# PSUM banks of the last two steps of the first stage, order of two copies, and due times of the output weights in an attention and spectral filter kernel

## The chip, the cores and the metric

The kernel runs on one core of one Trainium2 chip. The metric is the device time of one execution in microseconds (us). The engines are named as in the profile: PE multiplies matrices, PEld is its weight load, DVE is the vector engine, ACT the activation engine, POOL and SP issue most of the transfers (DMA); POOL computes a little too.

## The reference

Two independent halves, joined along the last axis. S = 2048, D = 448, 16 heads of 28, with one key and one value head for all:

```python
q = (x @ wq).reshape(B, S, H, Dh).transpose(0, 2, 1, 3)
k, v = x @ wk, x @ wv                       # one head of 28
p = softmax(einsum("bhqd,bkd->bhqk", q, k) * Dh ** -0.5)
a = einsum("bhqk,bkd->bhqd", p, v).transpose(0, 2, 1, 3).reshape(B, S, H * Dh) @ wo
X = rfft2(B_x, axes=(-2, -1)) * (w_r + 1j * w_i)
b = irfft2(X, s=(S, D), axes=(-2, -1))
out = concatenate([a, b], axis=-1)
```

## The kernel before

**First stage (0 to about 60 us).** The projections of queries, keys and values, and the first part of the spectral transform. Its tasks are declared with `add(engine, duration, function, *dependencies)`, and a small planner puts them in an order by these hand-written durations. [...] `spin(...)` hands out banks 0 to 5 in turn; banks 6 and 7 hold the two halves of the first transform (`fft1_mm`), which `fft1_evict` (L201) copies out, partly on ACT. The last two PE tasks of this stage are `turn_values_all` (16 transposes of the values, L616, into one bank) and `last_features` (L639; `features`, L184: the matmuls of the last features of the spectral block L = 3, two times 226 columns). PE then passes a branch on a register (L650), whose rare path widens the range of the numbers and is not taken here. Behind the branch DVE copies the turned values to `vs` (L722), makes the low half of the second half of the keys (`keys_low(1)`, L507; queue SP then copies them into place, L511), and copies the features to `late["a", 3]` (L726, a tile that the trace names `spoh`).

**Main loop.** 16 groups, one for each of 4 column chunks by 4 groups of heads, each of 16 steps over the keys: 256 steps. A step has two score units (`scores(i)`, L1326: 8 matmuls into two banks), two exponentials on ACT (L1329, 128 x 1024 each) and one value unit (`values(st)`, L1345: 8 matmuls that add into one bank). Score unit i uses the bank pair

```python
b = 2 * (2 * i % 3)          # L1321: banks 0/1, 4/5, 2/3, 0/1, ...
```

and the value unit of group n uses bank 7 − n % 2. The other of banks 6 and 7 is free for fillers. A filler is a piece of the spectral half or of the output product, put between units of attention when the kernel's own clocks allow: `late_features` (L1058), `late_points` (L1091), `late_top` (L1012), then `z_unit` (L1162), `y_unit` (L1188) and the output product (L1264). DVE copies each filler's bank out (L1067 and L1068, L1100 or L1102, L1017), and that sets when the bank is free for the next.

**Order of the side work.** `after(when, duration, function)` puts an event in a queue sorted by time on the kernel's own clock for DVE; `vector(until)` takes events out when they are due and emits their instructions. That clock is counted from the start of the main loop in assumed durations. Each engine and each DMA queue then runs its instructions strictly in the emitted order. The events that the change touches:

- `wo_load(g)` (L770): one part of the output weights by POOL's queue into one of two buffers; `wo_split(g)` (L773, and L775 for g < 4): its high and low half on DVE. Seven parts.
- `spread(i)` (L807): four transfers of the first spectral points into tile X, by POOL's queue; `first_points`: two reductions over X (L898, `peaks<-X`) and first butterflies (L822), some us later on DVE.

Beside them on POOL's queue: `weight_top` (L903, the spectral weights, whose largest value L898 takes), and for every finished group L1224 (sums to memory, after L1219 on DVE has taken them out of PSUM), L1225 (back in another layout, after the first has landed), L1230 and L1232 (their reciprocals, L1229, spread out).

Of the kernel before, what the change touches and what calls it, by code (L numbers as in the profile page):

```python
# [26 lines left out]
NG = 4  # L27
# [17 lines left out]
class Plan:  # L45
# [4 lines left out]
    def add(self, eng, dur, f, *deps, kb=0, due=None):  # L50
        t = {"eng": eng, "dur": dur, "f": f, "deps": [d for d in deps if d], "kb": kb, "due": due, "n": len(self.tasks)}
        self.tasks.append(t)
        return t
# [48 lines left out]
def kernel(ctx: ExitStack, tc: tile.TileContext, t: dict):  # L102
    nc = tc.nc
# [20 lines left out]
    bank = [banks[:, i] for i in range(8)]  # L124
    turn = count()

    def view(b, *dims):
        n = int(np.prod(dims))
        names = "abc"[:len(dims)]
        return b[:, :n].rearrange(f"p ({' '.join(names)}) -> p {' '.join(names)}", **dict(zip(names, dims)))  # L130

    def spin(*dims):
        return view(bank[next(turn) % 6], *dims)

    L = 3
    SEQ = 5, 6, 4, 7
    late, cs1 = {}, spare[1][1][:, :452].rearrange("p (j n) -> p j n", j=4)
# [40 lines left out]
    def features(pa, f, p, es=(0, 1)):  # L178
        for e in es:
            for k in range(2):  # L180
                for h in range(2):
                    for r in range(2):
                        r0 = 64 * h + 32 * r
                        mm(pa[r0:r0 + 32, e, 113 * k:113 * k + 113], f[:113, 2 * r + k, 2 * p + e, h], cs1[:113, 2 * r + k],  # L184
                           start=True, stop=True)
# [58 lines left out]
    with tc.tile_pool(name="f1", bufs=2) as f1[0], tc.tile_pool(name="w1", bufs=1) as w1, ExitStack() as ctx1:  # L244
# [10 lines left out]
        PE, DVE, ACT, SP, POOL = "PE", "DVE", "ACT", "SP", "POOL"  # L255
        add = plan.add

        kfz = add(POOL, 1.8, lambda: nc.gpsimd.memset(kf, 0.0))
        users = []
# [151 lines left out]
        fold, fa, ev_a, fm, outs, stores, xbl = {}, {}, {}, {}, {}, {}, {}  # L411
# [23 lines left out]
        pas = {}  # L435
# [18 lines left out]
        pbs, bst, store_tasks = {}, {}, {}  # L454
# [46 lines left out]
        def keys_cast(h, eng):  # L501
            hs = slice(h * 1024, h * 1024 + 1024)
            cast(eng, lambda: ka[:32, hs], lambda: kf[:32, hs])

        def keys_low(h):
            hs = slice(h * 1024, h * 1024 + 1024)
            nc.vector.tensor_tensor(ka[64:96, hs], kf[:32, hs], ka[:32, hs], op=ALU.subtract)  # L507

        def keys_twice(h, p):
            hs = slice(h * 1024, h * 1024 + 1024)  # L510
            nc.sync.dma_start(ka[64 * p + 32:64 * p + 64, hs], ka[64 * p:64 * p + 32, hs])  # L511
# [100 lines left out]
        turned = []  # L612

        def turn_values(bs):
            for b in bs:
                nc.tensor.transpose(turned[0][:, b], kf[32:64, b * 128:(b + 1) * 128], cons["ident"][32:64, 32:64])  # L616

        def turn_values_all():
            turned.append(next(turn) % 6)
            turned.insert(0, view(bank[turned[0]], 16, 32))  # L620
            turn_values(range(16))
            small["rv"] = nc.values_load(bits.bitcast(I32)[0:1, 0:1])
# [7 lines left out]
        def tops():  # L630
# [3 lines left out]
                         cm, ident_)  # L634
        fm_task(2)
        add(PE, 1.2, turn_values_all, users[-6], ident_, *krow_, *fetched["v"], bt_)
        users.append(None)

        def last_features():  # L639
            pas[L, 1] = spin(2, 226)  # L640
            features(pas[L, 1], ff[L], 1)
        add(ACT, 1.0, lambda: keys_cast(1, ACT), krow_[0], *fetched["k1"], bt_)
        add(PE, 0.8, last_features, users[-6], *store_tasks[L - 1])
        plan.run({PE: 4.4, DVE: 1.0, ACT: 2.0, SP: 0.6, POOL: 0.6})
        mask, ident = cons["mask"], cons["ident"]
        ctx1.close()
# [73 lines left out]


        nc.vector.tensor_copy(vs, turned[0])  # L722
        keys_low(1)
        for p in range(2):
            keys_twice(1, p)
        nc.vector.tensor_copy(late["a", L][:, 1], pas[L, 1])  # L726

    pp = ctx.enter_context(tc.tile_pool(name="pp", bufs=PAIRS))
    ap = ctx.enter_context(tc.tile_pool(name="ap", bufs=2))
# [10 lines left out]
    def after(when, dur, f, *a):  # L740
        heapq.heappush(events, (when, next(serial), dur, f, a))
# [609 lines left out]
            after(clk["pe"] + 0.4, 0.72, group_out, c, g)  # L1351

    for g in range(7):
        at = 24.0 + 6 * g if g < NG else 60.0 + 6 * g
        after(at, 0.0, wo_load, g)
        after(at + 6.0, 1.1, wo_split, g)

    last = acc(15)
    parts, tail = deque((k, g) for k in range(4) for g in range(NG - 1)), {}
# [10 lines left out]

    after(1.0, 0.0, largest)
    for i in range(4):
        after(30.0 + i, 0.0, spread, i)
    after(34.0, 0.0, first_points)
    after(20.0, 0.0, weight_top, 0)
    work["l"].extend([late_points(L, 0), late_points(L, 1)])
    late_load(0, "C")
# [49 lines left out]
    c, g = NC - 1, NG - 1  # L1427
# [150 lines left out]
```

## Time and profile before

| | |
|---|---|
| median of 3 runs | 580.16 us (580.13 to 581.7) |
| the profiled execution | 579.96 us |
| its span, first to last instruction | 578.2 us |
| mean granted clock of PE | 0.997 |
| main loop, first score matmul | 60.61 us |
| last value unit of the attention ends, by the chain of waits | 565.3 us |

The profile has one execution. Times in it are counted from the span's start. "Busy" leaves out waiting. In a group's line the number behind the second bar is the idle time of the engine ahead of these instructions, with what ended most of it. In a row of the timeline, the bracket is the idle time just ahead of it and its releaser. PEld runs beside PE, so its idle time is seldom a loss.

### The profile page before, as it was taken

The page shows a single profiled execution, that of the slowest core. Times are in us where ns is not written, and L with a number is a line of the kernel's source. Part 1 is how long each engine was busy: PE and PEld are TensorE (multiplying, and loading weights), DVE is VectorE, ACT ScalarE, POOL GpSimd, SP SyncE. Part 2 cuts the span into 40 slices and gives each one's busy share as a digit, 9 for nine tenths or more (in the row PEclk, how much of TensorE's full clock was granted, in tenths as well). Part 3 has the DMA queues.
Part 4 walks back from the last instruction along what each step waited for, and adds up shares of the span by engine and source line. Part 5 has one row for each costly group of instructions (what it writes and reads, how often), then busy time and mean ns, then how long its engine had stood idle before and what let it go on. Part 6 is the DMA issues. An engine that isn't in the chain of part 4 may idle for free.

```text
span 578.2 us, 21096 instructions
## 1 busy us (share of the span) xinstructions
PE 568.2 (98%) x9165; PEld 297.0 (51%) x9165; DVE 412.0 (71%) x779; ACT 510.1 (88%) x575; POOL 108.9 (19%) x199
## 2 busy tenths in 40 slices
PE   9999899899999999999999999999999999999997
PEld 7877344445554444444444444444555555554554
DVE  5994779799631899999899797873356743365566
ACT  4645799799999999999999999999999978899982
POOL 1024111122213012122111121032313212020200
PEclk9999899999999999999999999999999999999999
DMA  8843864424535302143411021267333323221112
GB/s 299 302 143 89 258 174 166 117 62 124 163 89 178 132 19 66 44 122 98 123 33 58 19 82 28 74 247 219 110 113 105 118 93 101 73 74 58 46 50 101
DMA packets 38359, 66.01 MB, mean 114 GB/s; under 512 B 6996, under 2 KB 28508, under 8 KB 38256
## 3 DMA queue, kind: packets, MB, share of 16 engines
q1 hardware_dynamic: 29432, 38.66, 20.7%
q0 software_dynamic: 8688, 25.76, 14.8%
q8 instruction: 72, 1.18, 0.8%
q14 instruction: 23, 0.19, 0.1%
q10 hardware_dynamic: 144, 0.23, 0.1%
HBM read 43.92 MB, written 19.97 MB: 111 GB/s over the span
## 4 chain that ended last, share of the span: by engine, by line
PE 83%; DVE 3%; DMA 1%; ACT 1%; issue 1%; POOL 0%; ACTq 0%; DVEq 0%; POOLq 0%
PE banks L1326 37%; PE banks L1345 36%; PE banks L1264 6%; PE banks L1162 2%; PE banks L1188 2%; PE banks L1091 1%; PE banks L1058 1%; DMA sd<-qraw 1%; DVE peaks L898 1%; ACT p L1329 1%; DMA wo<-wo 0%; DVE mt L1008 0%; ACT yb L1276 0%; DVE ka L507 0%; DVE spoh L1042 0%
## 5 line engine op out<-in xcount | busy, mean ns | idle before, releaser
L1329 ACT ACTIVATE p<-banks 128x1024 f32<-128x1024 f32 x512 | 476.5, 1085 | 27.7 <-PE banks L1326 26.4
L1326 PE MATMUL banks<-qa,ka 128*32 128x512 f16 x4096 | 275.0, 380 | 2.2 <-DVE spoh L726 2.2
L1345 PE MATMUL banks<-p,vs 128*32 128x512 f32 x2048 | 267.4, 592 | 0.3 <-DVE spol L1068 0.3
L1326 PEld LDWEIGHTS <-ka 128*32 128x32 f16 x4096 | 126.5, 97 | 168.6 <-issue 119.9
L1345 PEld LDWEIGHTS banks<-p,vs 128*32 128x32 f32 x2048 | 68.0, 110 | 44.4 <-issue 1.2
L1264 PE MATMUL banks<-woh,o 128*32 128x448 f16 x464 | 39.8, 352 | 0.0
L1232 POOL DMA_DIRECT2D R<-rd x60 | 30.3, 513 | 32.8 <-DMA rd<-rs 32.6
L1264 PEld LDWEIGHTS <-o 128*32 128x32 f16 x720 | 22.2, 97 | 27.1 <-issue 19.3
L864 DVE SCALAR_TENSOR_TENSOR X<-w,X 128x226 f32<-128x226 f32 (+2 forms) x72 | 34.0, 473 | 2.4
L1224 POOL DMA_DIRECT2D sd<-qraw x15 | 9.0, 598 | 126.9 <-DVE qraw L1219 126.9
L1269 DVE TENSOR_SCALAR ya<-banks,scales 128x448 f32<-128x448 f32 x12 | 8.2, 684 | 30.0 <-PE banks L1264 30.0
L1219 DVE TENSOR_SCALAR qraw<-banks,scales 128x512 f32<-128x512 f32 x15 | 11.2, 749 | 22.1 <-PE banks L1345 22.1
L1195 DVE TENSOR_SCALAR w<-banks,scales 128x256 f32<-128x256 f32 x16 | 7.7, 484 | 26.3 <-PE banks L1188 26.3
L1264 PE MATMUL banks<-wol,o 128*32 128x448 f16 x256 | 24.2, 352 | 0.0
L352 PE MATMUL banks<-xh,wqh 128*128 128x512 f32 x64 | 24.1, 408 | 0.0
L356 ACT ACTIVATE qraw<-banks 128x512 f32<-128x512 f32 x16 | 9.4, 598 | 16.3 <-PE banks L352 16.3
L352 PE MATMUL banks<-xh,wql 128*128 128x512 f32 x64 | 23.0, 390 | 0.0
L1230 POOL DMA_DIRECT2D rd<-rs x15 | 8.2, 550 | 75.5 <-DVE rs L1229 63.6
L822 DVE TENSOR_TENSOR X<-X 128x904 f32<-128x904 f32 (+2 forms) x10 | 9.1, 906 | 14.5 <-DMA X<-t 14.5
L857 DVE SCALAR_TENSOR_TENSOR w<-X 128x113 f32<-128x113 f32 (+2 forms) x56 | 17.5, 355 | 0.1
L352 PE MATMUL banks<-xl,wqh 128*128 128x512 f32 x48 | 17.2, 390 | 0.0
L938 DVE TENSOR_TENSOR w<-X,wf 128x904 f32<-128x904 f32 x16 | 16.9, 1094 | 0.2
(182 smaller groups left out, 560.6 us busy)
## 6 DMA issues: line engine op xcount, KB each, us to landing
qa<-qd SPq DMA_DIRECT2D x62, 128.0 KB
ob<-yo SPq DMA_DIRECT2D x16, 256.0 KB
t<-bs SPq DMA_DIRECT2D x16, 226.0 KB
w<-w POOLq DMA_DIRECT2D x8, 452.0 KB, 4.1
X<-t POOLq DMA_DIRECT2D x8, 452.0 KB, 5.8
wf<-w POOLq DMA_DIRECT2D x8, 452.0 KB, 3.7
x<-t POOLq DMA_DIRECT2D x8, 452.0 KB, 3.9
R<-rd POOLq DMA_DIRECT2D x60, 56.0 KB, 2.2
```

The source lines that it names most:

```text
L352: mm(pq[c, g], w[:, j, gs], x[:, j], start=(j == 0 and n == 0), stop=(j == 3 and n == 1))
L857: STT(out, y, sy, x, op0=ALU.mult, op1=ALU.add if c > 0 else ALU.subtract)
L864: todo(226 * n, lambda d=d, q=q: STT(both(d), t[0].rearrange("p r n f -> p r (n f)"), q, both(a), op0=ALU.mult, op1=ALU.add))
L938: TT(u[r], both(s), wt[k][:, r:r + 1].to_broadcast([128, 2, 452]), op=ALU.mult)
L1162: mm(pz[r, j], fb["c2", q % 2][:, x, e, j, r], fb["fi", q % 2][:, j, f], start=(n == 0), stop=(n == 2))
L1188: mm(py[m:m + 32, k].rearrange("p (j n) -> p j n", j=4), cs3[:w, kind, f, m:m + 32], fb["z", q % 2, e][:w, x, :, 64 * r:64 * r + 64], star ...
L1219: V.tensor_scalar(o, bank[b], scale_v, None, op0=ALU.mult)
L1232: nc.gpsimd.dma_start(R[32 * i:32 * i + DH], rd[i:i + 1].to_broadcast([DH, CW]))
L1264: mm(p[r:r + 32], x[c][:, g, s][:, r:r + 32], w[:, m], start=(g == 0 and n == 0), stop=(g == NG - 1 and n == 2))
L1326: mm(bank[b + h][r], ka[:, k:k + 32], qa[c, g][:, 2 * p + h], start=True, stop=True)
L1329: nc.scalar.activation(pt[i], banks[:, b:b + 2], AF.Exp, scale=SCALE / UP / UP)
L1345: mm(bank[b][32 * i:32 * i + 32], vs[:, kc], pt[2 * st + i // 2][:, i % 2], start=(kc == 0), stop=(kc == 15))
```

## The change

```diff
         def turn_values_all():
-            turned.append(next(turn) % 6)
+            turned.append(3)
             turned.insert(0, view(bank[turned[0]], 16, 32))
 ...
         def last_features():
-            pas[L, 1] = spin(2, 226)
+            pas[L, 1] = view(bank[7], 2, 226)
             features(pas[L, 1], ff[L], 1)
 ...
-        add(PE, 0.8, last_features, users[-6], *store_tasks[L - 1])
+        add(PE, 0.8, last_features, *outs[L - 1], *store_tasks[L - 1])
 ...
         nc.vector.tensor_copy(vs, turned[0])
+        nc.vector.tensor_copy(late["a", L][:, 1], pas[L, 1])
         keys_low(1)
         for p in range(2):
             keys_twice(1, p)
-        nc.vector.tensor_copy(late["a", L][:, 1], pas[L, 1])
 ...
     for g in range(7):
-        at = 24.0 + 6 * g if g < NG else 60.0 + 6 * g
-        after(at, 0.0, wo_load, g)
-        after(at + 6.0, 1.1, wo_split, g)
+        after(60.0 + 9 * g, 0.0, wo_load, g)
+        after(74.0 + 9 * g, 1.1, wo_split, g)
 ...
     for i in range(4):
-        after(30.0 + i, 0.0, spread, i)
-    after(34.0, 0.0, first_points)
+        after(36.0 + i, 0.0, spread, i)
+    after(40.0, 0.0, first_points)
```

The turned values take bank 3 (before: bank 5), and the last features take bank 7 (before: bank 0). `outs[L - 1]` are the copies (L201) that empty banks 6 and 7 of the transform before; the last features now come after them. The copy of the features is moved ahead of the keys' low half (L726 becomes L723). The output weights are loaded and split later on the kernel's clock and with 14 instead of 6 between load and split; the four transfers of X and what is done with them come 6 later. From there on the lines of the changed kernel are numbered one lower.

On DVE, just behind the branch, the difference is this (a plus is a row of the changed kernel, a minus one of the kernel before; names are out<-in):

```order
 L650 UNCONDITIONAL_BRANCH x2
 L722 COPY vs<-banks 128x512
+L723 COPY spoh<-banks 128x452
 L507 TENSOR_TENSOR ka<-kf,ka 32x1024
-L726 COPY spoh<-banks 128x452
 L748 MEMSET one 128x128
```

The copy of the features moved ahead of L507, and the memset still follows both.

On DVE, at the end of the first group (L1219 takes its sums out of PSUM), the difference of the two:

```order
 L1219 TENSOR_SCALAR qraw<-banks,scales 128x512
-L773 TENSOR_SCALAR woh<-wo,scales 128x448
-L775 SCALAR_TENSOR_TENSOR wol<-wo,scales,woh 128x448
 L166 TENSOR_TENSOR spoh<-x_911 113x16x32 x2
+L1100 TENSOR_SCALAR bs<-banks,tops 128x4x113
+L898 TENSOR_REDUCE peaks<-w 128x1
+L898 TENSOR_REDUCE peaks<-bs 128x1
+L168 TENSOR_TENSOR x_911<-spoh 113x512
+L169 TENSOR_TENSOR x_911<-spoh 113x512
 L1017 TENSOR_SCALAR tops<-banks 128x2
```

The split of the weights has left the place, and L1100, which empties a filler's bank, has come up to it. Before, that L1100 stood here, behind two more rows of the split and a reduction over X:

```order
L773 TENSOR_SCALAR woh<-wo,scales 128x448
L775 SCALAR_TENSOR_TENSOR wol<-wo,scales,woh 128x448
L168 TENSOR_TENSOR x_911<-spoh 113x512
L169 TENSOR_TENSOR x_911<-spoh 113x512
L898 TENSOR_REDUCE peaks<-X 128x1
L1100 TENSOR_SCALAR bs<-banks,tops 128x4x113
```

In the changed kernel the first reduction over X comes 16 rows behind that L1100, behind L1229, and ahead of the next L1067 and L1068:

```order
L1068 SCALAR_TENSOR_TENSOR spol<-banks,spol 128x452
L1039 TENSOR_SCALAR x_911<-spoh,tops 113x1024
L1229 RECIPROCAL rs<-rs 128x16
L898 TENSOR_REDUCE peaks<-X 128x1
L1067 TENSOR_SCALAR spol<-banks 128x452
L1068 SCALAR_TENSOR_TENSOR spol<-banks,spol 128x452
```

POOL's queue at the same place, before:

```order
L903 DMA w<-w 128x904
L770 DMA wo<-wo 128x448
L903 DMA w<-w 128x904
L770 DMA wo<-wo 128x448
L807 DMA X<-t_83 128x904 x4
L1224 DMA sd<-qraw 4x512
L1225 DMA rs<-sd 128x16
L770 DMA wo<-wo 128x448 x2
```

and in the changed kernel:

```order
L903 DMA w<-w 128x904 x2
L1224 DMA sd<-qraw 4x512
L1225 DMA rs<-sd 128x16
L807 DMA X<-t_83 128x904 x4
L903 DMA w<-w 128x904
L1230 DMA rd<-rs 128x16
L1232 DMA R<-rd 28x512 x4
```

The transfers of X have gone behind those of the first group's sums, and no load of output weights is left there.

## The prediction

> **What bounds the kernel now.** I read the page's shares first. TensorE (PE) is busy for 98% of the span; the groups of the two matmul lines and of the exponential show which engine it runs against:
>
> ```profile
> PE 568.2 (98%) x9165; PEld 297.0 (51%) x9165; DVE 412.0 (71%) x779; ACT 510.1 (88%) x575; POOL 108.9 (19%) x199
> ...
> L1329 ACT ACTIVATE p<-banks 128x1024 f32<-128x1024 f32 x512 | 476.5, 1085 | 27.7 <-PE banks L1326 26.4
> L1326 PE MATMUL banks<-qa,ka 128*32 128x512 f16 x4096 | 275.0, 380 | 2.2 <-DVE spoh L726 2.2
> L1345 PE MATMUL banks<-p,vs 128*32 128x512 f32 x2048 | 267.4, 592 | 0.3 <-DVE spol L1068 0.3
> ```
>
> In the whole main loop the scores (L1326) waited 2.2 us for another engine, once, and the values (L1345) 0.3 us, once. So time can only come from those waits, from the clock, or from fillers that wait. The view by windows (us, PE busy, PEld busy, DVE busy, ACT busy, POOL busy, granted clock, DMA share, GB/s) shows where PE is not full:
>
> ```profile
> 57.32:60.74 3.42, 1.25 (x40) 0.96 (x42) 2.68 (x4) 0.93 (x2) 1.16 (x2) 1.00 0.60 151
> 60.74:64.15 3.41, 3.41 (x36) 1.47 (x32) 0.00 (x0) 2.48 (x3) 1.65 (x3) 0.50 0.93 229
> 108.52:111.93 3.41, 1.54 (x20) 0.48 (x13) 3.41 (x5) 2.32 (x3) 0.00 (x0) 1.00 0.21 81
> 111.93:115.35 3.42, 2.82 (x84) 1.73 (x87) 3.38 (x8) 1.48 (x2) 0.00 (x0) 1.00 0.43 97
> 113.00:562.00 449.00, 449.00 (x7584) 221.20 (x7575) 315.60 (x591) 427.86 (x460) 85.41 (x154) 1.00 0.31 95
> 172.00:230.00 58.00, 58.00 (x816) 25.95 (x808) 41.34 (x69) 57.97 (x64) 13.63 (x25) 1.00 0.31 98
> ```
>
> From 113 to 562 us PE is busy throughout at full clock, so nothing that the change moves there can gain. Two places are left: 57 to 64 us, with a gap and then one stretch at clock 0.50, and 108 to 113 us. Between 172 and 230 ACT is full too: 64 exponentials in 57.97 us, 0.906 us each; PE's work for one is priced in part two. The waits from 60 to 120 us (total, times, longest) name the releasers:
>
> ```profile
> DVE woh L773 <- DMA wo<-wo: 4.1, 1, 4.1
> PE banks L1058 <- DVE bs L1100: 2.5, 1, 2.5
> PE banks L1326 <- DVE spoh L726: 2.2, 1, 2.2
> ```
>
> **Part one: the start of the main loop.** The timeline there, and the row of PE's branch at L650:
>
> ```profile
> 57.26 1.28 POOL L605 COPY qa<-ql 32x512 f16<-32x512 f16 x2 [0.93 <-issue]
> 57.27 0.99 ACT L201 ACTIVATE bs<-banks 128x452 f32<-128x452 f32 x2 [0.78 <-ACT ka L298]
> 57.46 0.99 PE L184 MATMUL banks<-spol,f 113*32 113x113 f32 x32
> 57.96 0.69 DVE L722 COPY vs<-banks 128x512 f32<-128x512 f32 x1 [2.15 <-DVEq L650]
> 58.68 1.22 DVE L507 TENSOR_TENSOR ka<-kf,ka 32x1024 f16<-32x1024 f32 x1
> 59.93 0.63 DVE L726 COPY spoh<-banks 128x452 f32<-128x452 f32 x1
> 60.61 2.68 PE L1326 MATMUL banks<-qa,ka 128*32 128x512 f16 x24 [2.17 <-DVE spoh L726]
> ```
>
> ```profile
> L650 PEldq EVENT_SEMAPHORE  x1: 51/51/51, 58.5 to 58.5; - x1
> ```
>
> Before, the last features (L184) lie in bank 0, which the first scores write, so these wait until L726, behind L722 and L507, has copied them out. Afterwards the features lie in bank 7 and the turned values in bank 3, and the copy is DVE's second. Scores 0 use banks 0 and 1 and need neither; scores 1 need banks 4 and 5; scores 2 (banks 2 and 3) come two units later and need L722, which is done at 58.65.
>
> The new cost: bank 7 still holds spectral points that ACT evicts with the second L201, ending at 58.26. The features, before at 57.46, therefore start at about 58.3 and end at 59.3. PE passed its branch at 58.5, right after its features ended at 58.45; so it passes it at about 59.35, and with some 0.35 for the first weight load and its start (an estimate: it must lie between 0 and the old first scores) scores begin at 59.7. POOL's last L605 copy, which they also need, ends at 58.54. Gain 0.9 us; between 1.3 (scores right at the features' end) and 0 (something else holds them to 60.6). DVE's copy of the features goes from 59.3 to about 60.0, and L507 from there to 61.2 instead of 59.9. What waits behind it, SP's second copy of the keys (L511) and POOL's loads (L781), is not due for the first 16 exponentials, some 14 us: cost nothing; were that cover gone, at most the 1.3 us.
>
> **Part two: the clock.** After the old gap of 2.17 us the clock is 0.50 for one stretch of 3.41 us. The chain of waits prices it, the same work slow and later fast:
>
> ```profile
> 60.61 2.68 PE banks L1326 x24
> 63.29 1.25 PE banks L1091 x16
> ...
> 66.26 0.86 PE banks L1326 x16
> 67.13 0.86 PE banks L1345 x8
> ...
> 75.36 0.76 PE banks L1091 x16
> ```
>
> At full clock eight score matmuls (one exponential's) take 0.43 us and a value step (two exponentials') 0.86, so PE needs 0.86 for each exponential, and 24 score matmuls take 1.29. The loss is 2.68 − 1.29 + 1.25 − 0.76 = 1.88 us, of which half of 3.41, 1.7, can be the clock; I take 1.7 and leave 0.18 for the pipeline's start. With the change PE idles 0.85 us ahead of the features and 0.4 behind them, so a stretch of 3.41 us holds about 2.2 of work, where 1.25 was followed by 0.50 and 1.54 (108.52) by 1.00. So the half clock should go: −1.7, bounds −1.9 and 0. [...]
>
> **Part three: the stall at 110 us.** DVE and POOL around it:
>
> ```profile
> 93.88 0.45 DVE L773 TENSOR_SCALAR woh<-wo,scales 128x448 f16<-128x448 f32 x1
> 94.96 0.62 DVE L1067 TENSOR_SCALAR spol<-banks 128x452 f16<-128x452 f32 x1
> ...
> 99.00 0.75 DVE L1219 TENSOR_SCALAR qraw<-banks,scales 128x512 f32<-128x512 f32 x1
> 100.04 0.60 POOL L1224 DMA_DIRECT2D sd<-qraw  x1 [10.54 <-DVE qraw L1219]
> 104.15 0.56 POOL L1225 DMA_DIRECT2D rs<-sd  x1 [3.51 <-DMA sd<-qraw]
> 104.70 1.06 POOL L770 DMA_DIRECT2D wo<-wo  x2
> 107.56 0.45 DVE L773 TENSOR_SCALAR woh<-wo,scales 128x448 f16<-128x448 f32 x1 [4.06 <-DMA wo<-wo]
> 109.85 2.03 DVE L898 TENSOR_REDUCE peaks<-X 128x1 f32<-128x1808 f32 x1
> 111.80 0.68 DVE L1100 TENSOR_SCALAR bs<-banks,tops 128x452 f32<-128x452 f32 x1
> ```
>
> POOL issued the third load of output weights at 104.70, behind L1225, which waits for a transfer. L773 on DVE waited 4.06 us for it, and L1100, which frees the filler bank, stood behind L773 and L898. PE's next filler (L1058) waited 2.5 us, as the waits above have it. In the new order the first points' L1100 stands right behind L1219 and L166, with no L773 ahead, and its L1091 comes five score pairs earlier. So −2.5 us. The 0.3 us of L1345 go as well: it waited for L1068, and the L773 with L775 ahead of L1067 held DVE for 94.96 − 93.88 = 1.08. Bounds −2.8 together, and 0 if it is only moved. All seven loads now stand 14 us ahead of their splits in the planner's time (before 6); the late one landed within 2.9 us of its issue. Their POOL issues, 0.53 us each (1.06 for two), leave their places ahead of L807 and go behind the first groups' L1224 to L1232; only L773 waits for them. The splits take as long as ever on a DVE that is busy 71%. I cost all that at nothing; without cover, one more wait like the 2.5.
>
> What is late next is X. Its four transfers (L807) used to stand ahead of L1224; now they stand behind L1224 and L1225. DVE follows PE here, 2.2 us earlier than before (0.9 + 1.7 − 0.4), so L1219 runs at 99.00 − 2.2 − 1.08 = 95.7, L1224 at 96.75, L1225 4.1 later at 100.85, and L807 from 101.4, the second at 101.95. From issue to landing L807 shows, as minimum, median and maximum from 60 to 180 us:
>
> ```profile
> DMA to landing us min/median/max: 3.9/5.3/6.8
> ```
>
> X's first half is there at 105.8, 107.2 or 108.7. Adding DVE's rows in the new order I get it to L898 of X at 106.5: a wait of 0, 0.7 or 2.2. Behind L898 come L1067 and L1068, which free a bank and make operands for PE's L1091 of score pair 56. Without a wait they end at 109.8; PE comes there at about 111.0, by 0.86 for each exponential, with the fillers (0.6 to 0.8) that now come sooner. So 1.2 us are to spare: loss 0 at the median, 1.0 at the longest. I take 0.
>
> **Part four: ACT.** If PE starts 0.9 earlier at full clock, the exponentials' 0.906 us against 0.86 let it wait until the first fillers fill in: about nine pairs by 0.046, 0.4 us, which I take; bounds 0 and 1.
>
> Sum: −0.9 − 1.7 − 2.5 − 0.3 + 0.4 = −5.0. The profiled execution took 579.96, 0.2 under the median of 580.16; I set the sum against the median: 575.2.
>
> **Rivals.** A, the forecast: 575.2. B, the half clock stays, because what lies ahead of the scores is mostly transposes and features of 113 columns, which may not count as work, or because the window falls badly: −3.3, 576.9. [...] For it: 57.32 to 60.74 held features too and did not count enough. Against: the idle share shrinks by nearly half. C, part of the stall comes back: X or a filler's eviction is late on DVE by 1 to 3 us beyond the 1.2 spare: 576.2 to 578. Against it: L1100's place; for it: the median landing already makes DVE wait. D, the change does not do what it says: the features' wait for ACT's L201 eats the start (0), the clock stays (0) and most of the stall only moves to the next DVE wait: 579 to 581, within 0.3%, that is 1.7 us, about what a measurement of this kernel can tell from no change. Three things must coincide. E, slower: L807 behind L1225. If sd lands late or the queue holds L807, DVE waits in L898 with everything behind it, and PE stops at pair 56. To lose the 5.0 and 1.7 more, X must land at 106.5 + 1.2 + 6.7 = 114.4, 12.4 us after its issue where 6.8 is the longest seen; then about 582.
>
> **Chances.** A 0.56, B 0.15, C 0.17, D 0.08, E 0.04. Faster: A, B and C with 0.88, less 0.01 for a C that reaches further: 0.87. Same 0.08, and 0.01 of C: 0.09. Slower 0.04. Low end: all bounds of the gains with no wait for ACT, −1.3 − 1.9 − 2.8 = −6.0, 574.2; I set 574.1. High end: B and most of a C, 577.6; beyond it lie D, E and a little of C. The forecast's own range is 574.1 to 576.2.
>
> **What would show it.** First L1326 at 59.7 with its wait named after L650 or L184, not L726; 24 of them in 1.3 us and clock 1.00 in every stretch behind 57 us; no "L1058 <- L1100" in the waits; L1100 near 98; L807 at 101 to 104 on POOL; and the last L1345 group about 5 us earlier. A clock of 0.50 after the first scores means B; an L898 that waits for X for more than 2 us with a PE wait behind it means C or E. A start at 60.6, or a PE gap elsewhere between 60 and 170 us, would make me wrong.

## The result and the profile after

The changed kernel takes 576.91 us (median of 7 runs, 576.1 to 578.18), the kernel before 580.13 in the same runs: ratio 0.994, 95% interval 0.9921 to 0.9959. That is 3.2 us or 0.6% less, clear of the noise since the interval lies below 1; it is within the range of the forecast but 1.7 above its number, and it is the time that rival B had. A second comparison gave 576.97 against 579.74, 0.9952 (0.9936 to 0.9967). The profiled execution took 577.14 with a span of 575.4.

The groups of the two attention lines, after (busy, mean ns, idle before and its releaser):

```profile
L1326 PE MATMUL banks<-qa,ka 128*32 128x512 f16 x4096 | 280.3, 381 | 1.0 <-issue 0.6 <-PEq L650 0.4
L1345 PE MATMUL banks<-p,vs 128*32 128x512 f32 x2048 | 271.2, 592 | 0.0
```

The waits for DVE are gone from both. What is left is 0.4 us behind the branch (PEq is PE's sequencer) and 0.6 us of "issue", in which PE waits for nothing that the profile shows. The stretches around the start, after (columns as in the prediction):

```profile
55.51:58.92 3.41, 2.47 (x56) 1.81 (x48) 0.75 (x2) 1.43 (x3) 1.52 (x3) 1.00 0.61 147
58.92:62.33 3.41, 3.17 (x30) 1.39 (x34) 1.96 (x3) 1.65 (x2) 0.88 (x2) 0.50 0.78 178
```

PE is now busy for 2.47 us of the first (before: 1.25), and the next one has clock 0.50 all the same. The timeline of the start:

```profile
55.81 1.18 PE L616 MATMUL banks<-ident,kf 32*128 32x32 f32 x16
57.74 0.99 PE L184 MATMUL banks<-spol,f 113*32 113x113 f32 x32 [0.75 <-ACT bs L201]
58.87 0.63 DVE L723 COPY spoh<-banks 128x452 f32<-128x452 f32 x1 [0.70 <-PEq L650]
59.13 0.16 PEld L1326 LDWEIGHTS <-ka 128*32 128x32 f16 x6 [0.65 <-issue]
59.16 3.12 PE L1326 MATMUL banks<-qa,ka 128*32 128x512 f16 x24 [0.43 <-PEq L650]
59.97 0.18 PEld L1326 LDWEIGHTS <-ka 128*32 128x32 f16 x8 [0.68 <-issue]
60.68 5.79 ACT L1329 ACTIVATE p<-banks 128x1024 f32<-128x1024 f32 x6 [2.99 <-PE banks L1326]
```

The features wait 0.75 us for ACT and the scores start 0.43 behind them, both as forecast. This execution had reached L616 0.54 us earlier than the one before (55.81 against 56.35), in work that the change does not touch. So I count from L616: first score 3.35 us behind it (before 4.26), but first exponential 4.87 (before 61.67 − 56.35 = 5.32). The weight loads pause from 59.18 to 59.97, in the middle of the first exponential's 8 matmuls. Around 110 us:

```profile
98.31 0.68 DVE L1100 TENSOR_SCALAR bs<-banks,tops 128x452 f32<-128x452 f32 x1
...
101.25 0.56 POOL L1225 DMA_DIRECT2D rs<-sd  x1 [3.17 <-DMA sd<-qraw]
101.80 2.13 POOL L807 DMA_DIRECT2D X<-t  x4
...
107.46 0.81 PE L1058 MATMUL banks<-spol,spoh 113*32 113x113 f16 x48
108.07 1.27 PE L1326 MATMUL banks<-qa,ka 128*32 128x512 f16 x18
108.87 2.04 DVE L898 TENSOR_REDUCE peaks<-X 128x1 f32<-128x1808 f32 x1 [1.22 <-DMA X<-t]
109.91 0.61 PE L1326 MATMUL banks<-qa,ka 128*32 128x512 f16 x6 [0.56 <-issue]
```

L1100 is there at 98.3 and no L1058 waits for it. L898 waits 1.22 us for X, and PE does not notice. But PE stands still for 0.56 us in the middle of score matmuls, with "issue" as its cause. A PE gap elsewhere between 60 and 170 us was one of the prediction's signs of being wrong. The lead over the execution before grew from 1.45 us at score unit 35 to 3.52 at unit 120. At 403 us 0.57 of it went, where L1162 came before DVE (L1269) had got to its bank, behind a late transfer:

```profile
401.91 0.69 DVE L1148 TENSOR_SCALAR c<-x,scales 128x904 f16<-128x904 f32 x1 [5.35 <-DMA x<-t]
403.71 0.68 DVE L1269 TENSOR_SCALAR ya<-banks,scales 128x448 f32<-128x448 f32 x1
404.44 0.85 PE L1162 MATMUL banks<-fi,c 128*32 128x128 f16 x48 [0.40 <-DVE ya L1269]
```

That transfer had not moved up with PE. The last score unit is 2.83 us earlier than before.

### The profile page after: what moved, and what is told of

Read it like the earlier page. It is cut to its first block, busy times and chain, and to the rows that moved or that the text cites. A ratio compares the mean times of both kernels' runs of the same rounds, so it can differ in the third digit from the quotient of the medians.

```text
span 575.4 us, 21096 instructions
## 1 busy us (share of the span) xinstructions
PE 568.0 (99%) x9165; PEld 307.8 (53%) x9165; DVE 412.0 (72%) x779; ACT 510.6 (89%) x575; POOL 109.3 (19%) x199
## 3 DMA queue, kind: packets, MB, share of 16 engines
q8 instruction: 72, 1.18, 0.8%
## 4 chain that ended last, share of the span: by engine, by line
PE 81%; DVE 4%; DMA 3%; issue 1%; ACT 0%; POOL 0%; POOLq 0%; ACTq 0%
PE banks L1326 36%; PE banks L1345 35%; PE banks L1264 5%; PE banks L1162 2%; DVE X L864 2%; PE banks L1188 2%; DMA t<-X 1%; DMA x<-t 1%; PE banks L1091 1%; PE banks L1058 1%; DVE w L857 1%; DVE w L859 0%; ACT yb L1276 0%; DVE c L1149 0%; DVE qraw L1219 0%
## 5 line engine op out<-in xcount | busy, mean ns | idle before, releaser
L1329 ACT ACTIVATE p<-banks 128x1024 f32<-128x1024 f32 x512 | 476.9, 1083 | 25.1 <-PE banks L1326 23.4
L1326 PE MATMUL banks<-qa,ka 128*32 128x512 f16 x4096 | 280.3, 381 | 1.0 <-issue 0.6
L1345 PE MATMUL banks<-p,vs 128*32 128x512 f32 x2048 | 271.2, 592 | 0.0
L1326 PEld LDWEIGHTS <-ka 128*32 128x32 f16 x4096 | 133.0, 97 | 162.4 <-issue 114.6
L1345 PEld LDWEIGHTS banks<-p,vs 128*32 128x32 f32 x2048 | 72.0, 110 | 41.7 <-issue 1.1
L1264 PEld LDWEIGHTS <-o 128*32 128x32 f16 x720 | 23.6, 97 | 25.3 <-issue 18.6
L1269 DVE TENSOR_SCALAR ya<-banks,scales 128x448 f32<-128x448 f32 x12 | 8.2, 683 | 31.8 <-PE banks L1264 31.8
L1219 DVE TENSOR_SCALAR qraw<-banks,scales 128x512 f32<-128x512 f32 x15 | 11.2, 748 | 20.8 <-PE banks L1345 20.7
```

The costliest lines, as they stand in the source:

```text
L1219: V.tensor_scalar(o, bank[b], scale_v, None, op0=ALU.mult)
L1264: mm(p[r:r + 32], x[c][:, g, s][:, r:r + 32], w[:, m], start=(g == 0 and n == 0), stop=(g == NG - 1 and n == 2))
L1326: mm(bank[b + h][r], ka[:, k:k + 32], qa[c, g][:, 2 * p + h], start=True, stop=True)
L1329: nc.scalar.activation(pt[i], banks[:, b:b + 2], AF.Exp, scale=SCALE / UP / UP)
L1345: mm(bank[b][32 * i:32 * i + 32], vs[:, kc], pt[2 * st + i // 2][:, i % 2], start=(kc == 0), stop=(kc == 15))
```

## Experiments

Every kernel was timed against the kernel before on the same chip, except where one execution is named; differences are taken from the ratios. "First exponential" is the start of the first L1329 minus the start of the first L616, from the trace.

**The parts alone.** Banks and copies only (the first three edits of the change):

> Only the banks and the place of the copy are changed, the output weights and X as before. If the trace after is read rightly, the first score matmul comes 0.9 us after where the first stage's own drift puts it (before: 4.26 us behind the first transpose L616, here about 3.35), the clock is 0.50 once behind it as before, and the stall of 2.5 us at 110 us stays: 0.9 us less than before, about 579.2. Rival: the new banks also end the half clock in this order, then 1.7 us more, about 577.5. Second rival: the gain of the whole change came from here, about 577.

578.59 us, ratio 0.9984 (0.997 to 0.9997): 0.9 us less, between 0.2 and 1.7. In its trace the first score came 3.38 us behind L616, as expected, the clock was 0.50 once, and the stall stayed:

```profile
PE banks L1058 <- DVE bs L1100: 2.8, 1, 2.8
```

But its first exponential came at 5.39, no earlier than before. PE paused between 59.70 and 60.77, behind six score matmuls.

Due times of weights and X only (the last two edits):

> Only the due times of the output weights and of X are changed, banks and copies as before. Expected: the wait of 2.2 us at the start stays, clock 0.50 once, L1058 no longer waits for L1100, a loss of 0.5 to 1 us elsewhere between 105 and 125 us stays: 1.6 to 2.5 us less than before, about 578. Rival: the stall only moves, no more than 0.5 us less, about 579.8.

577.18, ratio 0.9954 (0.9938 to 0.997): 2.7 us less. No L1058 waits for L1100 any more, and the 2.2 us for L726 are there. The two parts add up to 3.6; the whole gave 3.5 and 2.8 by its two ratios. Then only the output weights, X left ahead of the sums:

```diff
     for g in range(7):
-        at = 24.0 + 6 * g if g < NG else 60.0 + 6 * g
-        after(at, 0.0, wo_load, g)
-        after(at + 6.0, 1.1, wo_split, g)
+        after(60.0 + 9 * g, 0.0, wo_load, g)
+        after(74.0 + 9 * g, 1.1, wo_split, g)
```

> The kernel before with only the due times of the output weights changed (60 + 9 g and 74 + 9 g); X, banks and copies as before. X is then sent ahead of the first group's sums. If the wait of L773 for its late load was the cause of the stall, it is gone here too: 2.2 to 2.8 us less than before, about 577.1, like the kernel with both due times changed (577.2). Rival, that X behind the sums is what is needed: L898 of X, now ahead of L1067 on DVE, holds the filler banks, and less than 1.5 us is gained.

577.68, ratio 0.9958 (0.994 to 0.9975), 2.4 us less and the same as with X moved too. In its trace no L1058 waits for L1100, and L898 does not wait for X. The weights' due times took the stall away; where X goes made no difference that can be measured. And only the copy, in the old banks:

```diff
         nc.vector.tensor_copy(vs, turned[0])
+        nc.vector.tensor_copy(late["a", L][:, 1], pas[L, 1])
         keys_low(1)
         for p in range(2):
             keys_twice(1, p)
-        nc.vector.tensor_copy(late["a", L][:, 1], pas[L, 1])
```

> The kernel before with one edit: the copy of the features (L726) ahead of the keys' low half; banks 0 and 5, output weights and X as before. The copy then ends about 59.3 us (L616 at 56.35), so PE's wait falls from 2.2 to about 0.9 us, and the code behind the branch comes at about 59.9. Expected: as much as all of the bank change, 0.6 to 1.0 us less than before, about 578.8; the stall at 110 us stays. Rival, that the banks are needed: within 0.3 us of before, 579.5.

579.07, ratio 0.9996 (0.9981 to 1.0011): the expected 0.6 to 1.0 did not come. The trace shows why:

```profile
57.35 0.99 PE L184 MATMUL banks<-spol,f 113*32 113x113 f32 x32
59.24 0.61 PE L1326 MATMUL banks<-qa,ka 128*32 128x512 f16 x6 [0.91 <-DVE spoh L723]
60.95 1.47 PE L1326 MATMUL banks<-qa,ka 128*32 128x512 f16 x12 [1.10 <-issue]
```

The scores start 3.0 us behind L616, the earliest so far, and stop after six matmuls for more than a microsecond. The first exponential comes at 5.41.

**The clock.** Idle matmuls (on zeros, their result is not used) in the gap ahead of the last features of the changed kernel (20 in the second kernel):

```diff
             pas[L, 1] = view(bank[7], 2, 226)
+            for _ in range(6):
+                mm(bank[5][:, :256], idle[:, :128], idle[:, :256], start=True, stop=True)
             features(pas[L, 1], ff[L], 1)
```

> The changed kernel with 6 idle matmuls (128 x 256, 16 bit, zeros, into bank 5) between the transposes L616 and the last features, in the 0.75 us in which PE waits for ACT. Theory that the clock follows the matmul work in the window ahead: that window then holds about 3.1 us of 3.41 instead of 2.5, the clock stays 1.00 and the time is 1.5 to 1.9 us below the changed kernel's, about 575.1. Rival, that the transposes and the features of 113 columns hardly count: 0.65 us of full work is too little, the clock is 0.50 as before, 576.9. Second rival, that the idle matmuls delay the features: up to 0.6 us more, 577.5.

576.67, ratio 0.9948 (0.9929 to 0.9967). The clock was 1.00 throughout in the trace, and the mean clock 0.998 or more in all 8 runs:

```profile
55.60:59.01 3.41, 3.27 (x66) 2.32 (x57) 0.69 (x1) 1.47 (x3) 1.57 (x3) 1.00 0.62 147
59.01:62.43 3.42, 1.99 (x40) 1.13 (x44) 2.01 (x3) 1.26 (x2) 0.82 (x2) 1.00 0.77 173
```

So too little work in the stretch was the cause of the half clock. The 1.5 to 1.9 us did not come, though. The features were not late (1.95 us behind L616, 1.93 without the idle matmuls), but the scores now began 4.49 us behind L616 in place of 3.35, with PE idle for 1.56 us ahead of them, and the first exponential came at 5.22. The profile puts this idle time down to DVE's copy of the features; that copy had ended 0.79 us before, and in the changed kernel the scores start while it runs.

> The changed kernel with 20 such idle matmuls, about 2.1 us, so that the start is about 1.4 us later. If work in the window counts, the clock stays 1.00 and the main loop from first score on is 1.7 us shorter (first score to last value unit), with the time near 576.6. If the half clock comes from something else than too little counted work, it is still 0.50 and the time is about 578.3.

One execution: 578.12, clock 1.00, no pause at the start, first exponential 5.64. From the first exponential to score unit 10 it took 7.49 us, as with 6 idle matmuls; the changed kernel took 7.69 and the kernel before 8.30, each with one stretch at half clock. So behind a given first exponential one such stretch costs 0.2 to 0.8 us in these traces, since ACT, at 0.906 each, sets the pace at full clock. The second trace of the changed kernel (below) had two such stretches and took 9.00.

Whether transposes are what does not count:

```diff
-                nc.tensor.transpose(turned[0][:, b], kf[32:64, b * 128:(b + 1) * 128], cons["ident"][32:64, 32:64])
+                mm(turned[0][:, b], kf[32:64, b * 128:(b + 1) * 128], cons["ident"][32:64, 32:64], start=True, stop=True)
```

> The changed kernel with the 16 transposes of the values (L616) made as plain matmuls against the unit matrix, the rest the same. If transposes are what does not count as work for the clock, the stretch ahead of the first scores now holds over 2 us of counted work and the clock stays 1.00 in every window up to 570 us. If it is the total of work of any kind, nothing changes: 0.50 for one window near the first scores. Time within 0.5 us of the changed kernel's either way, 576.5 to 577.

One execution, 579.96, 3 us over the expected time, mainly because L616 took 4.21 us in place of 1.18: the trace has 32 matmuls for the 16 calls, where it had 16 transposes, and the last 1.1 us ran at half clock. The clock stayed low longer:

```profile
55.64:59.05 3.41, 3.41 (x36) 3.12 (x29) 0.00 (x0) 1.42 (x3) 1.50 (x3) 1.00 0.60 146
59.05:62.46 3.41, 2.98 (x42) 2.45 (x45) 1.21 (x2) 0.00 (x0) 0.00 (x0) 0.50 0.72 160
62.46:65.88 3.42, 3.42 (x36) 1.55 (x32) 1.49 (x3) 2.49 (x3) 1.35 (x3) 0.50 0.15 35
```

PE was busy for all of 3.41 us and the clock halved nevertheless. So busy time in the profile is not the measure; what L616 does with 32 columns on 32 rows was too little here as plain matmuls too.

**The pauses.** As I read the page, PE's instructions come in packets over a DMA queue of their own (queue 8): it brings 72 in the changed kernel, where PE has 9165 matmuls and 9165 weight loads, 255 for each packet. By then the pauses had two things in common: each ended 1.2 to 1.4 us after such a packet had landed, and each came at the same place, counted in PE's recorded instructions from the kernel's start. (The expectations call this the count of weight loads and matmuls; those alone are 1062 and 2846, and 1085 and 2877 count PE's recorded waits and its branch as well.) With the features in bank 2, free of the wait for ACT:

```diff
-            pas[L, 1] = view(bank[7], 2, 226)
+            pas[L, 1] = view(bank[2], 2, 226)
...
-        add(PE, 0.8, last_features, *outs[L - 1], *store_tasks[L - 1])
+        add(PE, 0.8, last_features, users[-6], *store_tasks[L - 1])
```

> The changed kernel with the last features in bank 2 and no wait for ACT's copies of bank 7, so that PE goes from L616 to the features without the 0.75 us gap. Theory that PE's code behind the branch is what comes last (in the runs so far PE goes on 1.2 to 1.4 us after the last packet of its instruction queue): the first scores come at most 0.5 us earlier, counted from L616, the main part of the 0.75 is lost in a pause of 0.5 us or more within or ahead of the first 8 score matmuls; with the ACT chain as pace from there on the time is 0 to 0.5 below the changed kernel's, 576.4 to 576.9. Rival, that only the features' place counts: 0.75 us less, 576.1, and no pause.

576.89, ratio 0.9956 (0.9939 to 0.9973), as the changed kernel. The scores began 2.53 us behind L616, 0.82 earlier than in the changed kernel where at most 0.5 was expected, and paused:

```profile
59.08 0.61 PE L1326 MATMUL banks<-qa,ka 128*32 128x512 f16 x6 [0.43 <-DVE vs L722]
60.90 1.35 PE L1326 MATMUL banks<-qa,ka 128*32 128x512 f16 x12 [1.21 <-issue]
```

The changed kernel once more, and two that move stores (L207) behind SP's branch, the second with the 6 idle matmuls:

```diff
+            if q == L - 1:
+                store_tasks[q] = list(outs[q])
+                return
             for e in range(2):
                 stores[q] = add(SP, 0.58, lambda e=e: fft1_store(q, bst[q], e), *outs[q], kb=226)
...
         for p in range(2):
             keys_twice(1, p)
+        for e in range(2):
+            fft1_store(L - 1, bst[L - 1], e)
```

> The changed kernel once more, beside the next two on one chip, and with a second trace. Expected: 576.9 against 579.5 (ratio 0.994 to 0.996). Theory that PE's instruction packets set the pauses: the second trace has its pause (if any) again where the recorded weight loads and matmuls count 1085 and 2877 from the kernel's start, and goes on 1.2 to 1.4 us after the end of the last packet on queue 8. Rival, chance waits for other engines: pauses at other places.

> The changed kernel with the two stores of block 2's points (L207, 226 KB each, on SP from about 57 to 59 us) issued behind SP's branch and the copies of the keys. Theory that PE's instruction packet comes late because it queues behind those stores: the packet starts within 1.4 us of L616's start (2.0 before), PE has no pause of 0.5 us at the first scores, the first exponential comes 0.4 to 0.7 us earlier counted from L616 (4.87 in the first trace), and the time is 0.3 to 0.7 below the changed kernel's. Rival, that the packet is asked for late, whatever the load: the packet again 2.0 us behind L616 and no gain (within 0.3).

> The same with the 6 idle matmuls ahead of the last features. If packet and clock are what the start lacks, the clock is 1.00, there is no pause at the first scores, the first exponential comes 3.35 + 0.75 = 4.1 us behind L616, 0.8 earlier than in the changed kernel, and the time is 0.8 to 1.0 below it, about 576. The 1.7 us of the forecast for the clock are not expected, since the exponentials at 0.906 us each then set the pace. Rival: with the packet still late, the gain stays under 0.4.

576.97 (0.9952), 576.77 (0.9946, 0.9928 to 0.9964) and 576.82 (0.9957, 0.994 to 0.9974). The changed kernel's second trace paused at 1085 as expected, and not at 2877. The stores are not what delays the packet: it starts 2.07 and 2.27 us behind L616 (1.95 and 2.41 in the two traces of the changed kernel), so both kernels missed their expectation and the rival held. In the second the trace had clock 0.50 once more in spite of the idle matmuls; in its 11 other runs the mean clock was 0.999 or 1.0. The stretch ahead of the half clock began in this trace at 58.22 us, when most of the idle matmuls (57.88 to 58.71) were done, and it held little:

```profile
58.22:61.63 3.41, 1.64 (x41) 1.05 (x42) 2.44 (x3) 0.46 (x2) 0.69 (x2) 1.00 0.24 56
61.63:65.05 3.42, 3.42 (x40) 1.53 (x36) 0.26 (x2) 2.57 (x3) 1.65 (x3) 0.50 0.52 79
```

The queue that carries the packets, in the changed kernel (packets, MB, share):

```profile
q8 instruction: 72, 1.18, 0.8%
```

That is 16 KB each. The single packets in the traces (times in us; "at count" is the last of PE's recorded instructions before the pause, counted from 0):

| kernel | packet ends | PE goes on | later by | at count |
|---|---|---|---|---|
| changed, first trace | 58.79 | 59.97 | 1.18 | 1085 |
| changed, second trace | 59.19 | 60.46 | 1.27 | 1085 |
| banks and copies only | 59.56 | 60.77 | 1.21 | 1085 |
| copy only | 59.72 | 60.95 | 1.23 | 1085 |
| 6 idle matmuls | 59.05 | 60.44 | 1.39 | 1085 |
| features in bank 2 | 59.57 | 60.90 | 1.33 | 1085 |
| late stores | 58.90 | 60.30 | 1.40 | 1085 |
| late stores, 6 idle | 60.18 | 61.46 | 1.28 | 1085 |
| changed, first trace | 108.48 | 109.91 | 1.43 | 2877 |
| 20 idle matmuls | 109.24 | 110.51 | 1.27 | 2877 |
| plain matmuls | 111.18 | 112.41 | 1.23 | 2877 |
| late stores | 108.78 | 110.14 | 1.36 | 2877 |
| late stores, 6 idle | 110.43 | 111.65 | 1.22 | 2877 |

The count stays although different instructions stand there (6 idle matmuls are 12 of the count), and 2877 − 1085 is 7 times 256; between the packets of these two places the queue brings seven. So 256 of PE's recorded instructions go with each 16 KB here. Most packets leave no such pause: behind 57 us the changed kernel's first trace shows one of over 0.5 us at two places, of the 72 packets in all. PE's only branch in that trace (L650) is at 58.0 us, and the second place, 2877, at 109. There two fillers of 48 short matmuls (L1058) stand three score units apart in the new order, in place of eight. With this order six of ten traces pause there (the last kernel below among them), and with another order none of four; that the fillers outrun the packet is an inference from this.

That made a prediction for a last kernel: with fewer instructions ahead of the scores, the place of the pause falls behind the first score unit.

```diff
-WARM = 8, 8
+WARM = 4, 4
...
-        idle = x1.tile([128, 256], BF16, name="idle", bufs=1)
+        idle = x1.tile([128, 512], BF16, name="idle", bufs=1)
...
-                mm(nothing[:, :256], idle[:, :128], idle, start=True, stop=True)
-        for _ in range(3):
-            mm(nothing[:, :128], idle[:, :128], idle[:, :128], start=True, stop=True)
+                mm(nothing, idle[:, :128], idle, start=True, stop=True)
+        mm(nothing[:, :384], idle[:, :128], idle[:, :384], start=True, stop=True)
...
+            for _ in range(3):
+                mm(bank[5], idle[:, :128], idle, start=True, stop=True)
             features(pas[L, 1], ff[L], 1)
```

> The changed kernel with the idle matmuls at the kernel's very start made half as many at twice the width (16 of 256 and 3 of 128 columns become 8 of 512 and 1 of 384: 20 instructions fewer, the same columns), and 3 idle ones of 512 columns ahead of the last features. So 14 instructions fewer stand ahead of the scores. If PE pauses wherever its instruction packet ends, the pause is again at the count of 1085 weight loads and matmuls, now behind the first unit of 8 score matmuls: the first exponential comes about 4.1 us behind L616 (4.87 and 5.40 in the two traces of the changed kernel), the clock is 1.00 throughout, and the time is 0.6 to 1.2 us below the changed kernel's 576.97, about 576.0. Rival, that the pause hangs on the branch and the first scores: it stays ahead of or within the first unit, the first exponential at 4.9 or later, and no gain (within 0.3).

575.51 us (575.07 to 576.53, 6 runs), ratio 0.9938 (0.9914 to 0.9961), clock 1.00 in the trace and 0.999 or 1.0 in every run. The start in its timeline (its lines are numbered a little otherwise, L615 for L616, L1327 for L1326, L1330 for L1329):

```profile
55.87 1.18 PE L615 MATMUL banks<-ident,kf 32*128 32x32 f32 x16
57.21 0.59 PE L641 MATMUL banks<-idle 128*128 128x512 bf16 x2 [0.16 <-issue]
57.83 0.98 PE L184 MATMUL banks<-spol,f 113*32 113x113 f32 x32
59.25 1.02 PE L1327 MATMUL banks<-qa,ka 128*32 128x512 f16 x13 [0.43 <-PEq L651]
59.98 6.62 ACT L1330 ACTIVATE p<-banks 128x1024 f32<-128x1024 f32 x7 [2.19 <-PE banks L1327]
60.55 0.83 PE L1327 MATMUL banks<-qa,ka 128*32 128x512 f16 x11 [0.27 <-issue]
```

The first exponential starts 59.98 − 55.87 = 4.11 us behind the transposes, as expected; the pause comes at a count of 1084, behind 13 score matmuls, 1.36 after the packet's end. At 2876 it pauses as well, again 1.36 us after the end of a packet (108.01). Against the changed kernel's 576.97 it is 1.5 us less by the medians, but in other runs, beside which the kernel before took 578.90 and not 579.74; by the ratios to it, 0.9938 and 0.9952, it is 0.8 us, and their intervals overlap. The time is the lowest of all kernels here; that it beats the changed kernel is likely and not settled.

## Why the prediction was right or wrong

**Start, −0.9.** Right for the first score (3.35 against 4.26 us behind L616, 0.91), and wrong as a gain. What counts is the first exponential, which needs 8 score matmuls first, and PE went on with those only 1.18 us after the end of an instruction packet (1.27 in the second trace): the first exponential came 0.45 us earlier in one trace of the changed kernel, 0.1 later in the other (5.40). The prediction bounded this term by "something else holds them" and named POOL's copy, not PE's own code. In the kernel before, the packet had ended at 58.76, within PE's wait of 2.2 us for the copy, and the scores began 1.85 us behind it, later than the 1.2 to 1.4 of the pauses. The experiment with banks and copies alone still gained 0.9 us (0.2 to 1.7) over its runs, which its one trace does not explain.

**Clock, −1.7.** This is the step that failed: "So the half clock should go". It stayed in both traces (twice as long in the second), and the mean clock was 0.997 or less in 16 of the 19 runs. The idle time did shrink, to 0.94 us of 3.41, but what I took for work, transposes and features, was not enough, and plain matmuls in the transposes' place did not hold the clock either. Rival B named that. The clock halved behind stretches with 2.47 and with 3.41 us busy of 3.41, and 0.6 to 0.8 us of wide matmuls kept the mean clock at 0.998 or more in 25 of 26 runs. So the lack of work ahead was the cause, and "busy" in the profile does not measure it. The price was oversized too. Within one kernel, features in bank 2, the four runs with a mean clock of 0.999 or 1.0 took 576.04 to 576.52 us and the eight others 576.80 to 578.25, a mean difference of 1.3 us. The kernel before has both kinds as well: in the later comparisons 71 of its 90 runs had 0.997 or less. There the runs at 0.996 or 0.997 were longer than those at 1.0 by 0.7 to 1.3 us on average, chip by chip. This sorts runs after their clock and is no experiment, but it puts the price of one stretch nearer 1 than 1.7.

**Stall, −2.5 and −0.3.** Right in cause: L773's late load, shown by moving the weights alone (−2.4 us), while X's place was free, as forecast. Between score units 35 and 120 the changed kernel gained 2.07 us of the 2.8 in its first trace. In its second, without the pause at 2877, it gained 2.67, and the same order in the kernel with due times only gained 2.69. So the 0.6 is that pause, which neither the profile's page nor the order of instructions shows as a wait.

**ACT, +0.4.** The right engine. Score unit 10 takes the banks of unit 7, whose exponential starts 7 x 0.906 = 6.3 us behind the first and takes 1.08 (the mean of its group): 7.4, and 7.49 was measured with the clock held. The term was thus too small beside a clock gain of 1.7: it is part of why a held clock alone gave almost nothing. Start, clock and ACT together were to give −2.2. From the first L616 to score unit 10 the kernel before took 13.62 us and the changed kernel 12.56 in its first trace and 14.40 in its second: 1.06 less and 0.78 more. Most of the measured 3.2 us is thus the stall.

**Rivals.** C and E did not come: L898 waited 1.22 us for X (0 to 2.2 was forecast), and no wait of PE followed. B named what happened to the clock, but that the time fell on its 576.9 is partly luck, since its other terms were off as well: the start gave less than 0.9, the stall 2.07 or 2.67 in place of 2.8. The 0.57 us at 403 are a wait behind a transfer that no term had; it was in the first trace of the changed kernel and not in its second or in that with 6 idle matmuls, so it comes and goes.

## What to carry to other kernels

A wait that is taken away can uncover the next thing that was late, and that need not be on any engine's list of waits (with the copy moved alone, PE's wait for it fell from 2.17 to 0.91 us, and 1.10 us of "issue" came behind it): look for "issue" pauses and compare their place, counted in instructions, over several traces. Count a gain at the engine that sets the pace (here the first exponential), not at the first instruction that moves. To hold the clock through a gap, a few wide idle matmuls (3.27 us busy of 3.41, then clock 1.00) did what narrow work that kept PE just as busy (3.41, then 0.50) did not; and 14 instructions fewer ahead of the scores moved the pause from behind 6 score matmuls to behind 13.

## What the hardware showed that was not expected

- PE goes on 1.2 to 1.4 us after the end of its 16 KB instruction packet, in 13 pauses at two places 7 x 256 recorded instructions apart. In 12 of them 0.7 to 2.0 us lie between the starts of two instructions; in the other, the weight loads alone pause, for 0.8 us.
- The granted clock halved after 3.41 us in which PE was busy throughout, 3.12 of it with matmuls of 32 columns, and did not after 1.54 us of attention matmuls. What exactly is counted stays open.
- 16 plain 32-bit matmul calls of 32 columns, 32 matmuls in the trace, took 4.21 us (1.1 of it at half clock) where the same 16 transposes took 1.18.
- What sets the start of the packet (1.35 to 2.6 us behind L616) stays open; moving 226 KB stores away from it changed nothing.
